# A fused sorted-attention and star-ReLU kernel: second query blocks loaded in f32 on the sync queue, last exps spread before their row sums

## Chip, cores and metric

One core of a Trainium2 chip runs the whole program. The metric is the device time in microseconds of one execution. The kernel before takes 223.7 us (median of three runs, 223.66 to 227.12).

## What is computed

Four batches with eight heads, 768 tokens in eight blocks of 96, head size 64. A small matrix per head (8x8) is normalised five times by exps, rows and columns; it mixes the blocks of keys and values. Each query block attends to its own mixed block. The result goes through a two-layer network with a squared ReLU.

```python
P = sort_net                                   # (4, 8, 8, 8)
for _ in range(5):
    P = exp(P - max(P, -1)); P /= sum(P, -1); P /= sum(P, -2)
k_sorted = einsum('bhij,bhjcd->bhicd', P, k_blocks)      # v the same
attn = softmax(q_block @ k_sorted_block.T / sqrt(64))
x = (attn @ v_sorted_block), heads joined       # 3072 x 512
h = x @ w_in                                   # 512 -> 2048
out = (s * relu(h)**2 + b) @ w_out             # 2048 -> 512
```

Inputs and output are f32. The kernel works in bf16 with f32 sums; the `b` term enters as a bias from the column sums of `w_out`.

## The kernel before

The order on each engine is written by hand: instructions run on an engine in the order in which the code records them, and waits are put in where tiles are shared. A half batch (384 tokens) is one network tile `t`; there are eight.

**The front** (L76 to L263). `sort_net` lies as 32 rows (batch and head) of 64. ACT takes the exps (L213), DVE the sums, reciprocals and products (L218 to L226); between them ACT moves f32 values into place (L183). In the fifth round the last step is the row product (L220); the column division is done later, in `take_p`. PE runs empty products meanwhile (`warm`, L176). `spread_p` (L234) then multiplies the 32 rows with a 0/1 matrix `emat`, so that each of 128 partitions (head, block, half) has its head's matrix: one product per batch, in f32, each two passes. `take_p` (L253) picks the partition's column with a mask, divides it by its sum, and `build_pd` (L275) makes the moving matrix `PD` of the mixing products. The copy `PB` keeps the other batches for later.

**Batch 0** (L550 to L578). `k_piece` (L290) makes 16 of 48 key columns a time: 32 products into a PSUM buffer, and one move to `KS` by ACT ("A") or DVE ("D"). `v_piece`, `q_piece` (transposes of query blocks 0 to 3), scores (`s_piece`), weighted values (`p_piece`) and transposes of x follow. PSUM has three double buffers (tag "a") and two single ones (tag "b"), taken in turn.

**GpSimd** issues nearly all loads, cast from f32 to bf16 on the way: keys, then query blocks 0 to 3 (`load_q(0, range(HB))`, L135), and after the masks are there `load_w` (L141):

```python
nc.gpsimd.tensor_copy(out=ones[:, 0:1], in_=PD[0][:, 0, 0, 0:1])   # holds GpSimd until PD is there
nc.gpsimd.memset(KS[1][:, :, :, C2:GAP], 0.0)
nc.gpsimd.memset(sel, 0.0)
part(0, 0)
nc.gpsimd.tensor_copy(out=ones[:, 0:1], in_=KS[0][:, 0, 0, C2 - 1:C2])  # until the keys are moved
part(0, 1); part(2, 0)
load_q(0, range(HB, NB))       # query blocks 4 to 7, four DMAs
part(2, 1)
```

`part(a, f)` loads rows `a`, `a+1` (of four groups of 128) and column quarter `f` of `w_in`; quarters 2 and 3 and four pieces of `w_out` follow. [...]

**The network** (`ffn1`, L484): for each pair of 128 hidden columns, part 0 and 1 of the four products, then ReLU on ACT (`rt`) and square on DVE (`gt`). `slots` says which other work stands where. In tile 0 (L641) three pairs are begun ahead; `("pre", 1)` and `1` hold `q_blocks` (L327): PE transposes of query blocks 4, 5 and 6, 7, moved by DVE and by ACT. They come ahead of the second half of pair 2, which needs `part(2, 1)`. `sel` and `part` (L584 to L589) are small masks that `sum_w` and `make_bias` use at tile 1.

**The sync engine** issues `sort_net`, four value loads, and from 54 us on transposes and stores.

Of the kernel before, what the change touches and what calls it, by code (L numbers as in the profile page):

```python
# [9 lines left out]
FP = mybir.dt.float32  # L10
BF = mybir.dt.bfloat16
AF = mybir.ActivationFunctionType
ALU = mybir.AluOpType
AX = mybir.AxisListType


def spread(t, dims):

    return bass.AP(tensor=t.tensor, offset=t.offset, ap=[list(t.ap[0])] + dims)
# [3 lines left out]
def kernel(  # L23
# [12 lines left out]
    nc = tc.nc  # L36

    B, H, S, D = q.shape
    NB = sort_net.shape[-1]
    BLK = S // NB  # L40
    BH = B * H
# [4 lines left out]
    HB = NB // 2  # L46
    TG = HB * BLK
    C2 = BLK // 2
# [5 lines left out]
    CK = 16  # L54
# [7 lines left out]
    const = ctx.enter_context(tc.tile_pool(name="const", bufs=1))  # L62
# [5 lines left out]
    rtp = ctx.enter_context(tc.tile_pool(name="rtp", bufs=3))  # L68
    gtp = ctx.enter_context(tc.tile_pool(name="gtp", bufs=2))
    osb = ctx.enter_context(tc.tile_pool(name="osb", bufs=3))  # L70
    psa = ctx.enter_context(tc.tile_pool(name="psa", bufs=3, space=bass.MemoryType.PSUM))
# [6 lines left out]
    sn = sne[:, 0:NB, :]  # L78
# [3 lines left out]
    for c in range(0, C2, CV):  # L82
        nc.sync.dma_start(out=v0f[:, c:c + CV, :].rearrange("p c d -> p (c d)"),
                          in_=raw[2][0][:, c * D:(c + CV) * D])
# [18 lines left out]
    QTOK = {}  # L103

    def load_q(b, ns=range(NB)):

        if b not in QTOK:
            QTOK[b] = rawp.tile([BLK, NB, H, D], BF, tag="rawq", name="qtok")
        qv = q[b].rearrange("h (n t) d -> t n h d", n=NB)
        for n in ns:  # L110
            nc.gpsimd.dma_start(out=QTOK[b][:, n], in_=qv[:, n])  # L111
# [5 lines left out]
    KS = [const.tile([128, NG, 2, GAP], BF, name=f"ks{i}") for i in range(2)]  # L117
# [17 lines left out]
    load_q(0, range(HB))  # L135
    ones = const.tile([128, 32], BF)
    sel = const.tile([128, 128], BF)
    wi = const.tile([128, NHP, d_ff], BF)
    wo = const.tile([128, NF, d_model], BF)

    def load_w():  # L141
        wiv = moe_w_in.rearrange("(a p) f -> p a f", p=128)
        fq = d_ff // 4

        def part(a, f):
            nc.gpsimd.dma_start(out=wi[:, a:a + 2, f * fq:(f + 1) * fq],  # L146
                                in_=wiv[:, a:a + 2, f * fq:(f + 1) * fq])


        nc.gpsimd.tensor_copy(out=ones[:, 0:1], in_=PD[0][:, 0, 0, 0:1])  # L150
        nc.gpsimd.memset(KS[1][:, :, :, C2:GAP], 0.0)
        nc.gpsimd.memset(sel, 0.0)
        part(0, 0)
        nc.gpsimd.tensor_copy(out=ones[:, 0:1], in_=KS[0][:, 0, 0, C2 - 1:C2])
        part(0, 1)
        part(2, 0)
        load_q(0, range(HB, NB))
        part(2, 1)
        for f in (2, 3):
            for a in (0, 2):  # L160
                part(a, f)
        wov = moe_w_out.rearrange("(f p) n -> p f n", p=128)
        for c in range(4):
            fs = slice(c * (NF // 4), (c + 1) * (NF // 4))
            nc.gpsimd.dma_start(out=wo[:, fs, :], in_=wov[:, fs, :])
# [6 lines left out]
    def warm(n, w=512):  # L172
        for _ in range(n):
            if not Z:
                Z.append(psb.tile([128, 512], FP, tag="b", name="z"))
            nc.tensor.matmul(out=Z[0][:, 0:w], lhsT=zeros[:, 0:128], rhs=zeros[:, 0:w],  # L176
                             start=True, stop=True)


    def permute(eng, src, cs=slice(0, C2), ds=slice(0, D)):  # L180
# [25 lines left out]
        for z in range(2)  # L206
# [1 line left out]
    nc.vector.tensor_reduce(out=rstat, in_=sn, axis=AX.X, op=ALU.max)  # L208
    nc.vector.tensor_tensor(out=sn, in0=sn, in1=rstat.broadcast_to([BH, NB, NB]),
                            op=ALU.subtract)  # L210
    warm(108, 142)
    for it in range(5):
        nc.scalar.activation(out=sn, in_=sn, func=AF.Exp)  # L213
        for c in {1: (0,), 2: (1,), 4: (2, 3)}.get(it, ()):
            permute(nc.scalar, v0f, slice(c * CV, (c + 1) * CV))
        if it >= 1:
            idle[it - 1]()
        nc.vector.tensor_reduce(out=rstat, in_=sn, axis=AX.X, op=ALU.add)  # L218
        nc.vector.reciprocal(out=rrec, in_=rstat)
        nc.vector.tensor_tensor(out=sn, in0=sn, in1=rrec.broadcast_to([BH, NB, NB]), op=ALU.mult)  # L220
        if it == 4:
            break
        nc.vector.tensor_reduce(out=rstat, in_=sne.rearrange("p i j -> p j i"),  # L223
                                axis=AX.X, op=ALU.add)
        nc.vector.reciprocal(out=rrec, in_=rstat)
        nc.vector.tensor_tensor(out=sn, in0=sn, in1=spread(rrec, [[0, NB], list(rrec.ap[1])]),  # L226
                                op=ALU.mult)
# [1 line left out]
    PD = {}  # L229
    PT = const.tile([128, B, NB], FP)  # L230
    RC = const.tile([128, B], FP)
    PB = const.tile([128, B - 1, NB, NB], FP)

    def spread_p(b0, n):  # L234

        pe = psa.tile([128, n, NB, NB], FP, tag="a", name="pe")
        for b in range(n):
            nc.tensor.matmul(out=pe[:, b].rearrange("p i j -> p (i j)"), lhsT=emat[:, b0 + b, :],
                             rhs=sn.rearrange("p i j -> p (i j)"), start=True, stop=True)
        return pe  # L240

    def masks_z():
        idz = ident.rearrange("p (z a e j) -> p z a e j", z=2, a=NHP, e=2)
# [9 lines left out]
    def take_p(b0, n, pe, sel):  # L253

        bs = slice(b0, b0 + n)
        tmp = rtp.tile([128, n * NB, NB], FP, tag=f"tmp{n}", name="tmp")
        nc.vector.tensor_tensor(out=tmp, in0=pe.rearrange("p b i j -> p (b i) j"),
                                in1=spread(sel, [[0, n * NB], list(sel.ap[1])]), op=ALU.mult)
        nc.vector.tensor_reduce(out=PT[:, bs].rearrange("p b i -> p (b i)"), in_=tmp, axis=AX.X,
                                op=ALU.add)  # L260
        cs = rtp.tile([128, n], FP, tag=f"cs{n}", name="cs")
        nc.vector.tensor_reduce(out=cs, in_=PT[:, bs], axis=AX.X, op=ALU.add)
        nc.vector.reciprocal(out=RC[:, bs], in_=cs)  # L263
# [26 lines left out]
    def k_piece(b, c0, eng):  # L290
        src, mov, dst = RAW["k", b], PD[b], KS[b % 2]
        ps = psa.tile([128, CK, 2, NG], FP, tag="a", name="tp")
        for c in range(CK):
            for e in range(2):
                nc.tensor.matmul(out=ps[e * 64:(e + 1) * 64, c].rearrange("p z g -> p (z g)"),  # L295
                                 lhsT=src[:, c0 + c, :],
                                 rhs=mov[:, e].rearrange("p z g -> p (z g)"),
                                 start=True, stop=True)
        if b > 1:
            dst = dst.rearrange("p g z c -> p g (z c)")[:, :, 0:BLK].rearrange(  # L300
                "p g (z c) -> p g z c", z=2)
        evac(eng, dst[:, :, :, c0:c0 + CK], ps.rearrange("p c z g -> p g z c"))
# [181 lines left out]
    def ffn1(t, slots, ahead=0):  # L484

        gt = gtp.tile([128, NF, TG], BF, tag="gt", name="gt")
        GT[t] = gt
        xt = XT[t]
        H1 = {}

        def part(i, hpl):
            if i not in H1:
                H1[i] = psa.tile([128, 2, 512], FP, tag="a", name="hps")
            for f in range(2):
                for hp in hpl:
                    fc = (2 * i + f) * 128
                    nc.tensor.matmul(out=H1[i][:, f, 0:TG], lhsT=wi[:, hp, fc:fc + 128],  # L497
                                     rhs=xt[:, :, hp, :],
                                     start=(hp == 0), stop=(hp == NHP - 1))

        for i in range(ahead):
            for p in slots.get(i - ahead, ()):
                p()
            part(i, (0, 1))
        for i in range(NF // 2):
            part(i, (2, 3) if i < ahead else range(NHP))
            for p in slots.get(("pre", i), ()):
                p()
            rt = rtp.tile([128, 2, TG], BF, tag="rt", name="rt")
            h = H1.pop(i)[:, :, 0:TG]  # L510
            nc.scalar.activation(out=rt, in_=h, func=AF.Relu)  # L511
            nc.vector.tensor_tensor(out=gt[:, 2 * i:2 * i + 2, :], in0=rt, in1=rt, op=ALU.mult)  # L512
            for p in slots.get(i, ()):
                p()
# [32 lines left out]
        nc.sync.dma_start(out=out[r0:r0 + 128, ns], in_=ot[:, ns])  # L547


    take_p(0, 1, spread_p(0, 1), jsel)  # L550
    build_pd(0)
    pe = spread_p(1, B - 1)
    nc.vector.tensor_copy(out=PB, in_=pe)
    warm(3)
    k_piece(0, 0, "A")
    k_piece(0, CK, "D")
    k_piece(0, 2 * CK, "A")
    load_w()
    v_piece(0, 0, "A")
    q_piece(0, 0, "D")  # L560
# [23 lines left out]
    part = const.tile([128, 2], FP)  # L584
    nc.gpsimd.memset(part, -1.0)
    for r in range(0, 128, 32):
        nc.gpsimd.memset(sel[r:r + 3], 1.0)
        nc.gpsimd.memset(part[r:r + 1, 0:1], 0.0)
        nc.gpsimd.memset(part[r:r + 2, 1:2], 0.0)  # L589
    nc.gpsimd.memset(VO, 1.0)  # L590
# [44 lines left out]
    def TP(b, h, i, eng): return lambda: t_piece(b, h, i, eng)  # L635
    def TD(b, h): return lambda: t_dma(b, h)
    def PDB(b): return lambda: build_pd(b)
    def QB(b, n0, eng): return lambda: q_blocks(b, n0, eng)


    ffn1(0, {-1: [TP(0, 0, 2, "AD")], ("pre", 1): [QB(0, HB, "D")], 1: [QB(0, HB + 2, "A")],  # L641
             2: [SB(0, 1, 0)], 3: [SB(0, 1, 1), P(0, 1, 0)], 4: [SB(0, 1, 2), P(0, 1, 1)],
             5: [SB(0, 1, 3), P(0, 1, 2)], 6: [TP(0, 1, 0, "D"), P(0, 1, 3)]}, ahead=3)
    ffn1(1, {-2: [TP(0, 1, 2, "D")], 1: [masks_z, lambda: take_p(1, B - 1, PB, jselz), PDB(1)], 4: [PDB(2), sum_w],
# [20 lines left out]
    for b in range(B):  # L665
        n = b + 1
# [55 lines left out]
```

## Time and profile before

| | us |
|---|---|
| median of three runs | 223.7 |
| the profiled execution, its own time | 224.31 |
| its span, first to last instruction | 222.5 |
| PE busy | 214.8 (97%) |
| DVE / ACT / GpSimd busy | 116.6 / 100.8 / 55.2 |
| first key product on PE | 12.79 |
| transposes of query blocks 4 to 7 on PE | 26.67 to 27.5 |
| second half of pair 2, tile 0 | 28.44 |
| last `wo` piece seen landed | 43.7 |

The span is that of one profiled execution; the rest of its own time lies before the first and after the last instruction that the profile shows. PE is busy nearly all the time at its full granted clock, so the share alone says only that little is left; where PE waits is read from the timeline. The GpSimd queue's loads and their times, from issue until the landing is seen:

| load | issued | landed after |
|---|---|---|
| `part(0, 0)` | 14.04 | 4.0 |
| `part(0, 1)` | 16.15 | 5.9 |
| query blocks 4 to 7 | 17.55 to 20.6 | 6.0 to 6.5 |
| `part(2, 1)` | 20.62 | 7.8 |
| pieces of `wo` | 25.0 to 29.4 | 11.1 to 15.0 |

The column "DMA" of a queue's share is the sum of the times of its packets over 16 engines; packets overlap, so it can exceed 100%.

### The profile page before, as it was taken

The page shows a single profiled execution, that of the slowest core. Times are in us where ns is not written, and L with a number is a line of the kernel's source. Part 1 is how long each engine was busy: PE and PEld are TensorE (multiplying, and loading weights), DVE is VectorE, ACT ScalarE, POOL GpSimd, SP SyncE. Part 2 cuts the span into 40 slices and gives each one's busy share as a digit, 9 for nine tenths or more (in the row PEclk, how much of TensorE's full clock was granted, in tenths as well). Part 3 has the DMA queues.
Part 4 walks back from the last instruction along what each step waited for, and adds up shares of the span by engine and source line. Part 5 has one row for each costly group of instructions (what it writes and reads, how often), then busy time and mean ns, then how long its engine had stood idle before and what let it go on. Part 6 is the DMA issues. An engine that isn't in the chain of part 4 may idle for free.

```text
span 222.5 us, 5383 instructions
## 1 busy us (share of the span) xinstructions
PE 214.8 (97%) x2307; PEld 127.1 (57%) x2307; DVE 116.6 (52%) x237; ACT 100.8 (45%) x132; POOL 55.2 (25%) x99
## 2 busy tenths in 40 slices
PE   7898889999999999999999999999999999999993
PEld 8886556655555545655555545665455566654453
DVE  6857547599938556443426746444244734442122
ACT  4688476565442326663354136664325055650000
POOL 8349787359030009100040019000000000000000
PEclk9999999999999999999999999999999999999999
DMA  5999999999979769999669869969423240001212
GB/s 178 258 95 131 163 203 207 219 193 132 177 137 219 147 165 122 156 112 211 160 134 202 209 155 141 151 133 207 114 78 72 102 111 4 0 0 47 94 50 94
DMA packets 66744, 30.51 MB, mean 137 GB/s; under 512 B 57440, under 2 KB 61920, under 8 KB 66528
## 3 DMA queue, kind: packets, MB, share of 16 engines
q0 software_dynamic: 30832, 12.85, 47.3%
q1 hardware_dynamic: 35888, 17.31, 34.4%
q8 instruction: 18, 0.29, 0.5%
q14 instruction: 6, 0.05, 0.1%
HBM read 29.63 MB, written 8.65 MB: 172 GB/s over the span
## 4 chain that ended last, share of the span: by engine, by line
PE 86%; DMA 4%; DVE 4%; POOL 2%; ACT 2%; issue 1%; POOLq 0%
PE ops L522 36%; PE hps L497 36%; DMA wi<-in_moe_w_in_dram 3%; PE pv L441 3%; PE tp L295 2%; PE sc L406 2%; PE ops L536 2%; POOL qtok L111 1%; PE tv L379 1%; ACT ks L284 1%; DMA sne<-in_sort_net_dram 1%; POOL wi L146 1%; PE vob L360 1%; ACT sne L213 1%; DVE rstat L223 1%
## 5 line engine op out<-in xcount | busy, mean ns | idle before, releaser
L497 PE MATMUL hps<-xt,wi 128*128 128x384 bf16 x512 | 86.4, 326 | 1.3 <-DMA wi<-in_moe_w_in_dram 0.9
L522 PE MATMUL ops<-wo,gt 128*128 128x512 bf16 x368 | 84.9, 379 | 0.0
L511 ACT ACTIVATE rt<-hps 128x768 bf16<-128x768 f32 x64 | 51.6, 811 | 52.9 <-PE hps L497 52.0
L497 PEld LDWEIGHTS <-wi 128*128 128x128 bf16 x512 | 48.9, 98 | 35.4 <-issue 2.5
L512 DVE TENSOR_TENSOR gt<-rt 128x768 bf16<-128x768 bf16 x64 | 38.4, 602 | 44.0 <-ACT rt L511 41.9
L522 PEld LDWEIGHTS <-gt 128*128 128x128 bf16 x368 | 34.0, 98 | 37.6
L544 DVE SCALAR_TENSOR_TENSOR ot<-ops,s_bc,bias 128x512 f32<-128x512 f32 (+2 forms) x26 | 18.4, 706 | 33.5 <-PE ops L522 31.5
L411 ACT ACTIVATE at<-sc 96x768 bf16<-96x768 f32 (+1 forms) x28 | 21.2, 806 | 28.4 <-PE sc L406 28.4
L111 POOL DMA_DIRECT2D qtok<-in_q_dram x32 | 24.8, 786 | 7.5 <-DMA wo<-in_moe_w_out_dram 3.7
L449 DVE TENSOR_TENSOR x<-pv,rec 96x512 bf16<-96x512 f32 x32 | 22.0, 687 | 1.1
L441 PEld LDWEIGHTS <-at 112*128 112x128 bf16 (+3 forms) x256 | 10.9, 101 | 4.3 <-ACT vs L284 0.9
L441 PE MATMUL pv<-vs,at 112*128 112x66 bf16 (+3 forms) x256 | 11.7, 195 | 0.8 <-DVE vs L286 0.8
L176 PE MATMUL z<-zeros 128*128 128x142 bf16 (+1 forms) x114 | 11.0, 268 | 1.2 <-DVE zeros L115 1.2
L448 DVE RECIPROCAL rec<-pv 96x8 f32<-96x8 f32 x32 | 6.3, 198 | 11.2 <-PE pv L441 11.2
L284 ACT CAST ks<-tp 128x1024 bf16<-128x1024 f32 x8 | 8.1, 1012 | 7.4 <-PE tp L295 7.4
L176 PEld LDWEIGHTS <-zeros 128*128 128x128 bf16 x114 | 9.5, 116 | 1.4 <-DVE zeros L114 1.0
L661 POOL COPY gate<-gt 128x1 bf16<-128x1 bf16 x2 | 0.4, 191 | 36.8 <-DVE gt L512 36.8
L406 PEld LDWEIGHTS <-ks 64*128 64x128 bf16 x224 | 5.2, 94 | 5.1 <-issue 2.1
L286 DVE CAST ks<-tp 128x1024 bf16<-128x1024 f32 x4 | 4.9, 1222 | 5.7 <-PE tp L295 5.7
L406 PE MATMUL sc<-qt,ks 64*128 64x96 bf16 x224 | 7.5, 204 | 0.2 <-DVE x L449 0.2
L295 PEld LDWEIGHTS <-rawk 128*64 128x64 bf16 x384 | 6.4, 113 | 1.7 <-issue 1.3
L295 PE MATMUL tp<-pd,rawk 128*64 128x64 bf16 x384 | 6.8, 196 | 0.0
(105 smaller groups left out, 117.9 us busy)
## 6 DMA issues: line engine op xcount, KB each, us to landing
out_dram<-ot SPq DMA_DIRECT2D x23, 256.0 KB, 2.1
qtok<-in_q_dram POOLq DMA_DIRECT2D x32, 96.0 KB, 7.2
rawk<-in_k_dram POOLq DMA_DIRECT2D x6, 384.0 KB, 10.3
rawv<-in_v_dram POOLq DMA_DIRECT2D x6, 384.0 KB, 6.6
dv<-VO SPq DMA_DIRECT2D x12, 192.0 KB, 6.4
vs<-dv SPq DMA_DIRECT2D x2, 1152.0 KB, 7.2
wi<-in_moe_w_in_dram POOLq DMA_DIRECT2D x8, 256.0 KB, 8.1
wo<-in_moe_w_out_dram POOLq DMA_DIRECT2D x4, 512.0 KB, 13.8
```

Of the source, the lines that this page charges most:

```text
L111: nc.gpsimd.dma_start(out=QTOK[b][:, n], in_=qv[:, n])
L176: nc.tensor.matmul(out=Z[0][:, 0:w], lhsT=zeros[:, 0:128], rhs=zeros[:, 0:w], start=True, stop=True)
L295: nc.tensor.matmul(out=ps[e * 64:(e + 1) * 64, c].rearrange("p z g -> p (z g)"), lhsT=src[:, c0 + c, :], rhs=mov[:, e].rearrange("p z g -> ...
L406: nc.tensor.matmul(out=sc[:, e, n * BLK:(n + 1) * BLK], lhsT=KS[b % 2][pr, g0 + n].rearrange("p z c -> p (z c)"), rhs=QT[b][pr, half * HB ...
L411: nc.scalar.activation(out=at, in_=sc[0:rows(b), :, 0:TG], func=AF.Exp, scale=scale)
L441: nc.tensor.matmul(out=pv[0:m, e, n * VW:(n + 1) * VW], lhsT=atf[:, c0:c0 + m], rhs=VS[b > 1][:, e * NG + g0 + n, 0:VW], start=True, stop= ...
L449: nc.vector.tensor_tensor(out=x[:, :, hp * 128:(hp + 1) * 128].rearrange("p n (e d) -> p e n d", e=2), in0=pvv[:, :, :, 0:D], in1=rec.unsq ...
L497: nc.tensor.matmul(out=H1[i][:, f, 0:TG], lhsT=wi[:, hp, fc:fc + 128], rhs=xt[:, :, hp, :], start=(hp == 0), stop=(hp == NHP - 1))
L511: nc.scalar.activation(out=rt, in_=h, func=AF.Relu)
L512: nc.vector.tensor_tensor(out=gt[:, 2 * i:2 * i + 2, :], in0=rt, in1=rt, op=ALU.mult)
L522: nc.tensor.matmul(out=ops, lhsT=gt[:, f, m * 128:(m + 1) * 128], rhs=wo[:, f, :], start=(f == 0), stop=(f == NF - 1))
L544: nc.vector.scalar_tensor_tensor(out=ot[:, ns], in0=ops, scalar=s_bc, in1=BIAS[0][:, ns], op0=ALU.mult, op1=ALU.add)
```

## The change

Four things are changed together.

1. In the fifth round the row product is dropped. The exps themselves are spread as soon as ACT has made them, for all batches; the reciprocals of the row sums are spread by further products (`spread_r`) into a ninth row of the same PSUM buffers, and `take_p` multiplies by them. `PB` keeps nine rows. Four fewer empty products run before.
2. Query blocks 4 to 7 are loaded in f32, by four DMAs on the sync engine's queue, into a new tile `q0f`. A GpSimd memset of a part of `q0f`, after `part(0, 1)`, is what these DMAs wait for. Two DVE casts write the bf16 tile; they stand in slot -1 of tile 0, after the transposes of x.
3. GpSimd no longer waits for the moved keys between `part(0, 0)` and `part(0, 1)`; the four row memsets of `sel` move ahead of `part(0, 0)`.
4. The first three key moves go to DVE, ACT, DVE, where they went to ACT, DVE, ACT.

```diff
+    q0f = const.tile([BLK, HB, H, D], FP)
...
         nc.gpsimd.memset(sel, 0.0)
+        for r in range(0, 128, 32):
+            nc.gpsimd.memset(sel[r:r + 3], 1.0)
         part(0, 0)
-        nc.gpsimd.tensor_copy(out=ones[:, 0:1], in_=KS[0][:, 0, 0, C2 - 1:C2])
         part(0, 1)
+        nc.gpsimd.memset(q0f[:, :, 0, 0:1], 0.0)
+        qv = q[0].rearrange("h (n t) d -> t n h d", n=NB)
+        for n in range(HB):
+            nc.sync.dma_start(out=q0f[:, n], in_=qv[:, HB + n])
         part(2, 0)
-        load_q(0, range(HB, NB))
         part(2, 1)
...
-    warm(108, 142)
+    warm(104, 142)
...
-        nc.vector.tensor_tensor(out=sn, in0=sn, in1=rrec.broadcast_to([BH, NB, NB]), op=ALU.mult)
         if it == 4:
             break
+        nc.vector.tensor_tensor(out=sn, in0=sn, in1=rrec.broadcast_to([BH, NB, NB]), op=ALU.mult)
...
+    def spread_r(b0, n, pe):
+        for b in range(n):
+            nc.tensor.matmul(out=pe[:, b, NB], lhsT=emat[:, b0 + b, :], rhs=rrec,
+                             start=True, stop=True)
...
-        nc.vector.tensor_reduce(out=PT[:, bs].rearrange("p b i -> p (b i)"), in_=tmp, axis=AX.X,
-                                op=ALU.add)
+        pt = rtp.tile([128, n, NB], FP, tag=f"pt{n}", name="pt")
+        nc.vector.tensor_reduce(out=pt, in_=tmp, axis=AX.X, op=ALU.add)
+        nc.vector.tensor_tensor(out=PT[:, bs], in0=pt, in1=pe[:, :, NB], op=ALU.mult)
...
-    take_p(0, 1, spread_p(0, 1), jsel)
+    pe0 = spread_p(0, 1)
+    pe = spread_p(1, B - 1)
+    spread_r(0, 1, pe0)
+    spread_r(1, B - 1, pe)
+    take_p(0, 1, pe0, jsel)
     build_pd(0)
-    pe = spread_p(1, B - 1)
     nc.vector.tensor_copy(out=PB, in_=pe)
     warm(3)
-    k_piece(0, 0, "A")
-    k_piece(0, CK, "D")
-    k_piece(0, 2 * CK, "A")
+    k_piece(0, 0, "D")
+    k_piece(0, CK, "A")
+    k_piece(0, 2 * CK, "D")
...
-        nc.gpsimd.memset(sel[r:r + 3], 1.0)
...
+    def cast_q(n):
+        nc.vector.tensor_copy(out=QTOK[0][:, HB + n:HB + n + 2], in_=q0f[:, n:n + 2])
...
-    ffn1(0, {-1: [TP(0, 0, 2, "AD")], ("pre", 1): [QB(0, HB, "D")], 1: [QB(0, HB + 2, "A")],
+    ffn1(0, {-1: [TP(0, 0, 2, "AD"), lambda: cast_q(0), lambda: cast_q(2)], ("pre", 1): [QB(0, HB, "D")], 1: [QB(0, HB + 2, "A")],
```

More of the change, by code (lines that the diff above doesn't have):

```diff
@@ L231 @@
     RC = const.tile([128, B], FP)
-    PB = const.tile([128, B - 1, NB, NB], FP)
+    PB = const.tile([128, B - 1, NB + 1, NB], FP)
     def spread_p(b0, n):
-        pe = psa.tile([128, n, NB, NB], FP, tag="a", name="pe")
+        pe = psa.tile([128, n, NB + 1, NB], FP, tag="a", name="pe")
         for b in range(n):
-            nc.tensor.matmul(out=pe[:, b].rearrange("p i j -> p (i j)"), lhsT=emat[:, b0 + b, :],
+            nc.tensor.matmul(out=pe[:, b, 0:NB].rearrange("p i j -> p (i j)"), lhsT=emat[:, b0 + b, :],
                              rhs=sn.rearrange("p i j -> p (i j)"), start=True, stop=True)
         return pe
+    def spread_r(b0, n, pe):
+        for b in range(n):
+            nc.tensor.matmul(out=pe[:, b, NB], lhsT=emat[:, b0 + b, :], rhs=rrec,
+                             start=True, stop=True)
     def masks_z():
@@ L255, in take_p @@
         bs = slice(b0, b0 + n)
-        tmp = rtp.tile([128, n * NB, NB], FP, tag=f"tmp{n}", name="tmp")
-        nc.vector.tensor_tensor(out=tmp, in0=pe.rearrange("p b i j -> p (b i) j"),
-                                in1=spread(sel, [[0, n * NB], list(sel.ap[1])]), op=ALU.mult)
-        nc.vector.tensor_reduce(out=PT[:, bs].rearrange("p b i -> p (b i)"), in_=tmp, axis=AX.X,
-                                op=ALU.add)
+        tmp = rtp.tile([128, n, NB, NB], FP, tag=f"tmp{n}", name="tmp")
+        nc.vector.tensor_tensor(out=tmp, in0=pe[:, :, 0:NB],
+                                in1=spread(sel, [[0, n], [0, NB], list(sel.ap[1])]), op=ALU.mult)
+        pt = rtp.tile([128, n, NB], FP, tag=f"pt{n}", name="pt")
+        nc.vector.tensor_reduce(out=pt, in_=tmp, axis=AX.X, op=ALU.add)
+        nc.vector.tensor_tensor(out=PT[:, bs], in0=pt, in1=pe[:, :, NB], op=ALU.mult)
         cs = rtp.tile([128, n], FP, tag=f"cs{n}", name="cs")
```

## The prediction

> **What bounds the kernel now.** I read first the engine table and the slices (PE busy 97%, granted clock full everywhere), then the chain of waits, then the timeline around each place where PE stands, then the DMA queues in one-microsecond windows. The chain, in order of time, passes here (start us, length us, what):
>
> ```profile
> 11.04 1.07 PE pe L238 x8
> ...
> 15.69 0.19 POOL ones L154
> ...
> 16.15 1.42 POOL wi L146 x2
> 17.57 3.06 POOL qtok L111 x4
> 20.62 7.77 DMA wi<-in_moe_w_in_dram
> ```
>
> From 28.4 us to the end it is almost only PE. So there are two places to gain: the front up to the first key products, and the 0.93 us in which PE waits for the weight quarter `part(2, 1)` that GpSimd issues behind four query loads. Anything that makes PE wait after that is paid in full. The timeline shows what stands there (start, length, engine, line, operation; in brackets idle time and its releaser):
>
> ```profile
> 24.87 0.36 DVE L286 COPY xt<-tr 128x384 bf16<-128x384 bf16 x1 [0.52 <-PE tr L469]
> 26.67 0.85 PE L333 MATMUL tqb<-ident,qtok 96*128 96x96 bf16 x16
> 27.06 0.56 DVE L512 TENSOR_TENSOR gt<-rt 128x768 bf16<-128x768 bf16 x1 [1.84 <-ACT rt L511]
> 28.44 0.82 PE L497 MATMUL hps<-xt,wi 128*128 128x384 bf16 x4 [0.93 <-DMA wi<-in_moe_w_in_dram]
> ```
>
> PE transposes the second query blocks at 26.67. In the changed kernel that transpose stands behind two DVE casts, and they behind four loads on the sync queue. So the question is when those loads land. It is answered by how the two queues share the 16 DMA engines. These are the queue lines of four windows of 1 us, from 6, 29, 85 and 88 us (packets, MB, share of 16 engines; q0 is GpSimd's queue, q1 the sync engine's):
>
> ```profile
> q0 software_dynamic: 57, 0.12, 61.3%
> q1 hardware_dynamic: 57, 0.18, 47.7%
> ...
> q0 software_dynamic: 192, 0.18, 115.8%
> ...
> q1 hardware_dynamic: 886, 0.17, 89.6%
> ...
> q0 software_dynamic: 445, 0.06, 84.3%
> q1 hardware_dynamic: 452, 0.09, 77.1%
> ```
>
> At 6 us (key pieces against the f32 value load) and at 88 us (query rows against the rows stored for v) both queues are busy, and each gets the same number of packets although their sizes differ. The windows at 121 and 122 us, with 6 KB packets on q0 and 2 KB on q1, show 37 against 31 and 28 against 30. So they take turns packet by packet, and a queue with small packets gets few bytes beside one with large packets.
>
> [...] at 88 us a q1 packet takes 77.1% x 16 us / 452 = 27 ns, against 89.6% x 16 / 886 = 16 ns alone at 85 us, so nearly every single packet meets one of the other queue. [...] The nearest row here, the cast of 128x512 f32 at 48.77 us, took 0.43[...].
>
> **Queries on the sync queue (decides).** Removed from GpSimd: four issues, 3.06 us, ahead of `part(2, 1)`. Added on the sync engine: four issues, about 0.43 us each (the f32 value loads), behind a small GpSimd memset, and on DVE two casts. Nothing waits on the sync queue behind them until the key and query transposes at 53.9 us.
>
> When do they start? GpSimd's first weight issue was at 14.04; four small memsets of `sel` come ahead of it (0.20 each as a row at 29.50, partly overlapped: 0.6 to 0.8), the front moves it by -0.2 to 0 (below): 14.6. Two issues of 0.71 follow back to back, since the `KS` gate is gone, then the memset: 16.2. Sync issues at 16.3; its first packets come 0.6 us (the v rows, issued 82.87, running at 83.5) to 1.8 us after (the value load, issued 1.2, at full rate from 3.0). I take 17.5.
>
> How long? Before, the same query rows were 768 packets a load (24,576 of q0's 30,832 packets are 32 such loads). In f32 they are still runs of 64 elements, so four loads are 3,072 packets, 192 on each engine. GpSimd's queue meanwhile holds eight weight parts of 256 packets and four of `wo` with 512: 256 on each engine, so it does not run dry. One turn is a weight packet and a query packet. A weight packet alone costs 16 us / 192 = 83 ns, a small sync packet alone 16 us / 886 = 18 ns: 101 ns. From above, their durations beside each other: 115.8% x 16 / 192 = 97 and 27, 124 ns. At 6 us the turn of 16 / 57 = 281 ns lay between these two ways of counting (172 + 134 = 306). I take 105 ns. 192 turns are 20.2 us (19.4 to 23.8). The last load ends at 37.7, and is seen about 0.8 us later (value loads: last packets near 9.5 us, landing at 10.3): **38.5 us**. The first two are seen near 28.4.
>
> What waits? Both casts stand on DVE ahead of the first `gt` product (27.06), of the evacuation of the transposed queries (27.54) and of the second `gt`. Had the data been there by 25.2, they would lie in DVE's 1.84 us of idle time and cost nothing[...]. As it is, the second ends at 39.2. PE, in order, stands at the second `tqb` of eight transposes (0.42 us), and behind it part 2 of ffn1, which began at 28.44 and now begins at 39.7: **+11.2 us**, with the old 0.93 us wait swallowed. ACT and DVE are free to catch up in PE's stall, the rest behind it is PE's own chain, so nothing is given back. GpSimd's next loads keep their place: the same DMA engines have carried the same read bytes by then, and the batch-1 queries, issued from 41.77 before, also wait for `tqb` at 39.7.
>
> Bounds: if one engine's gaps let query packets through (q0 moved only 117 to 148 packets per us at 16 to 27 us, against 192 to 214 later), up to 9 us are saved; at 124 ns a turn, 3.6 us are added.
>
> **Front.** The row product (0.21 us) and its wait leave the path: PE waits for the exps, which end at 10.19, not for 10.90, so the first `pe` comes at about 10.34 instead of 11.04 (`warm` at 104 ends at 9.9). But `spread_r` stands behind all eight passes of `spread_p` (1.0 us), so the reciprocals arrive near 11.65, and one more product of 128x8 (about 0.16, the reduction of that size) follows: masks some 0.2 us earlier. Against it PE runs eight more passes (0.12 each, 1.0 us if the weight loads set the pace) and then `warm(3)`, 0.8 us: the key products start near 13.05 instead of 12.79. The swap gives the first key move to DVE (1.23 us against 1.01), which frees the buffer that the first v products wait for later: +0.2. Sum +0.3 to +0.5, bounded by -0.4 (if the passes overlap) and +0.7. All of it lies in the shadow of the query wait and costs nothing; without that wait it counts. `PB` has 24 columns more and the later `take_p` one op more (0.18 us on DVE at 45 us), beside PE work: nothing, at worst 0.2.
>
> **Sum.** Profiled span 222.5 + 11.2 = 233.7; its own time 224.31 + 11.2 = 235.5. That run lies 0.6 us above the median of 223.7, from which 234.9 follows: I say **235**.
>
> **Rivals.** *Hidden*: the queues share by bytes or time, or sync packets go in bunches. Four loads of 0.8 MB against an equal share of weights end 5 us after the start, by 24 us; the casts fit in the idle time, `part(2, 1)` lands 3 to 4 us earlier and PE's 0.93 us wait goes, the front gives back 0.3 to 0.5: 223.2 (222.5 to 224), not slower. [...] against it: the equal counts. It decides if the loads land before about 26 us. *Gaps*: the slow rate at 16 to 27 us means that engines wait for descriptors, and the other queue fills in; landing at 28 to 33, +1 to +6: 225 to 230. For it: the rates above; against: the slowest of 16 engines ends a load, and one without gaps is enough. *Front only*: the early spread does nothing because PE is in order; with hidden queries 223.7 + 0.4 - 0.9, within the first rival's range.
>
> **Chances.** One for one 0.80 (own range 230 to 239), gaps 0.07, hidden 0.13. The range 227 to 239 holds the first but for its ends and half of the second: about 0.8. Two per cent, 4.5 us, is what a measurement of this kernel can tell from no change (its three runs span 1.5%). Slower by over 2% is one-for-one and a little of gaps: 0.81. Within 2%: 0.18. Faster would need 219.2, below what PE's own work leaves (214.8 busy in 222.5 and 0.93 to win): 0.01.
>
> **What would show it.** A DVE wait of more than 10 us ahead of the casts, released by the q0f loads; PE idle until near 39 us; equal packet counts of both queues from 18 to 38 us, with q1 near 150 packets per us; q0f landing 10 to 20 us after issue. It is wrong if q1 shows several times q0's count in that stretch, or if the first relu products keep their time at 27 us. The front is right if the first key product starts at 12.6 to 13.1.

## The result, and the profile after

The changed kernel takes **243.35 us** (median of six runs, 240.6 to 246.86), the kernel before 224.62 beside it (223.48 to 227.12). The runs of the changed kernel lie near 241 or near 246, and every ratio here compares the shorter runs of both kernels: 1.072, interval 1.064 to 1.081. That is some 16 us more; forecast were 11 us more, 235, and a range up to 239. The direction was right, the size was 5 us too small by this ratio.

The profiled execution's own time is 245.52, its span 243.7; against it the forecast was 10 us too small. Of its profile these are the span, the engines' busy time, the PE slices with the granted clock, and the two DMA queues:

```profile
span 243.7 us, 5396 instructions
...
PE 219.3 (90%) x2311; PEld 128.8 (53%) x2311; DVE 120.0 (49%) x241; ACT 100.0 (41%) x131; POOL 51.8 (21%) x95
...
PE   8797411994999999999999999999999999999994
...
PEclk9999955598999999999999999999999999999999
...
q0 software_dynamic: 27696, 12.46, 40.5%
q1 hardware_dynamic: 39024, 18.10, 34.1%
```

The same two rows of the kernel before:

```profile
PE   7898889999999999999999999999999999999993
...
PEclk9999999999999999999999999999999999999999
```

PE does 4.5 us more of busy time and still falls from 97% to 90%. A slice is 6.1 us. Slices 5 to 7 of the PE row (4, 1, 1) are one hole from about 27 to 42 us, and the clock row reads 5 in slices 6 to 8: half speed, where the kernel before has 9, full speed, throughout. Slice 10 has a second, smaller dip in both rows. The chain of waits shows what the hole is (start us, length us, what; the SPq rows are the sync engine's issues):

```profile
16.88 0.11 POOL q0f L158
...
17.01 0.34 SPq L161
...
17.40 0.54 SPq L161
...
17.98 2.67 SPq L161
...
20.69 20.47 DMA q0f<-in_q_dram
...
41.19 0.70 DVE qtok L656
...
41.93 0.82 PE tqb L345 x8
```

Before, the chain passed here through GpSimd's issues and a weight quarter, and came out at 28.4. Now it is the last of the four query loads, one transfer of 20.5 us. The sync engine took 2.67 us for the third issue and 5.02 for the fourth, where 0.43 was expected. The timeline shows both casts, and a second place where PE stands:

```profile
31.25 1.76 DVE L656 CAST qtok<-q0f 96x1024 bf16<-96x1024 f32 x1 [5.51 <-DMA q0f<-in_q_dram]
41.19 0.69 DVE L656 CAST qtok<-q0f 96x1024 bf16<-96x1024 f32 x1 [8.18 <-DMA q0f<-in_q_dram]
...
33.07 0.82 PE L345 MATMUL tqb<-ident,qtok 96*128 96x96 bf16 x8 [5.72 <-DVE qtok L656]
41.93 0.82 PE L345 MATMUL tqb<-ident,qtok 96*128 96x96 bf16 x8 [8.05 <-DVE qtok L656]
42.55 1.48 PE L509 MATMUL hps<-xt,wi 128*128 128x384 bf16 x4
...
54.35 3.77 DVE L524 TENSOR_TENSOR gt<-rt 128x768 bf16<-128x768 bf16 x1 [0.56 <-ACT rt L523]
54.58 3.11 POOL L190 COPY VP<-rawv 128x384 bf16<-128x384 bf16 x4
...
58.64 1.46 PE L509 MATMUL hps<-xt,wi 128*128 128x384 bf16 x4 [3.26 <-DVE xt L298]
```

The brackets carry the reading: DVE waits 5.5 and 8.2 us for the loads, PE 5.7 and 8.05 us for the casts, and the second half of pair 2 starts at 42.55 where it started at 28.44. It stands behind the transposes in the code and waits there although what it reads was there long before: the last `xt` piece was copied by 25.74, and all quarters of `wi` had landed by 33.4 (last issue 20.4, longest landing 13.0). The last three lines are a loss that the prediction did not have: a `gt` product that takes about 0.56 us elsewhere takes 3.77, lies beside GpSimd's moves of `VP`, and holds up the DVE copy `xt` behind it, for which PE waits 3.26.

The account of the added span, by stage. Beside it stands the profile of **e2**, which has the query part of the change alone; that execution took 240.99:

| us | changed kernel | e2 |
|---|---|---|
| second half of pair 2 starts later | 14.1 (42.55 - 28.44) | 14.2 (42.62 - 28.44) |
| the next two pairs at half clock (3.02 before) | 2.4 (5.41) | 1.1 (4.13) |
| PE waits behind a `gt` held up by GpSimd | 3.3 | 1.5 |
| half clock once more behind that wait (7.02 before) | 1.6 (8.59) | none |
| sum | 21.4 | 16.8 |
| span less 222.5 | 21.2 | 16.7 |

The second row compares 42.55 to 47.96 (e2: 42.62 to 46.75) with 28.44 to 31.46 before, the fourth 58.64 to 67.23 with 38.80 to 45.82 before. The first row is the same in both columns. The next three are 7.3 us in one profile and 2.6 in the other; what sets the two executions apart is not shown.

### The profile page after: what moved, and what is told of

The parts are those of the page before. It is cut to its first block, busy times and chain, and to the rows that moved or that the text cites. A ratio compares the mean times of both kernels' runs of the same rounds, so it can differ in the third digit from the quotient of the medians.

```text
span 243.7 us, 5396 instructions
## 1 busy us (share of the span) xinstructions
PE 219.3 (90%) x2311; PEld 128.8 (53%) x2311; DVE 120.0 (49%) x241; ACT 100.0 (41%) x131; POOL 51.8 (21%) x95
## 3 DMA queue, kind: packets, MB, share of 16 engines
q0 software_dynamic: 27696, 12.46, 40.5%
q1 hardware_dynamic: 39024, 18.10, 34.1%
## 4 chain that ended last, share of the span: by engine, by line
PE 80%; DMA 9%; DVE 5%; ACT 1%; SPq 1%; POOL 1%; issue 1%; POOLq 0%
PE hps L509 34%; PE ops L534 33%; DMA q0f<-in_q_dram 8%; PE pv L453 3%; PE sc L418 2%; PE tp L307 2%; DVE gt L524 2%; SPq L161 1%; PE ops L548 1%; PE tv L391 1%; DMA sne<-in_sort_net_dram 1%; ACT VP L188 1%; PE scb L433 1%; POOL wi L147 1%; PE vob L372 1%
## 5 line engine op out<-in xcount | busy, mean ns | idle before, releaser
L509 PE MATMUL hps<-xt,wi 128*128 128x384 bf16 x512 | 89.8, 334 | 3.5 <-DVE xt L298 3.3
L509 PEld LDWEIGHTS <-wi 128*128 128x128 bf16 x512 | 50.0, 100 | 39.1 <-issue 5.0
L556 DVE SCALAR_TENSOR_TENSOR ot<-ops,s_bc,bias 128x512 f32<-128x512 f32 (+2 forms) x26 | 18.4, 706 | 33.8 <-PE ops L534 31.5
L423 ACT ACTIVATE at<-sc 96x768 bf16<-96x768 f32 (+1 forms) x28 | 21.2, 805 | 28.4 <-PE sc L418 28.4
L111 POOL DMA_DIRECT2D qtok<-in_q_dram x28 | 21.6, 783 | 8.7 <-DVE gt L524 2.5
L345 PE MATMUL tqb<-ident,qtok 96*128 96x96 bf16 x16 | 1.6, 278 | 13.8 <-DVE qtok L656 13.8
L460 DVE RECIPROCAL rec<-pv 96x8 f32<-96x8 f32 x32 | 6.3, 196 | 11.2 <-PE pv L453 11.2
L181 PE MATMUL z<-zeros 128*128 128x142 bf16 (+1 forms) x110 | 9.8, 254 | 1.2 <-DVE zeros L115 1.2
L296 ACT CAST ks<-tp 128x1024 bf16<-128x1024 f32 x7 | 7.1, 1012 | 8.2 <-PE tp L307 8.2
L298 DVE CAST ks<-tp 128x1024 bf16<-128x1024 f32 x5 | 6.0, 1223 | 6.6 <-PE tp L307 6.6
L656 DVE CAST qtok<-q0f 96x1024 bf16<-96x1024 f32 x2 | 2.4, 1224 | 13.7 <-DMA q0f<-in_q_dram 13.7
L181 PEld LDWEIGHTS <-zeros 128*128 128x128 bf16 x110 | 8.3, 109 | 1.4 <-DVE zeros L114 1.0
L345 PEld LDWEIGHTS <-qtok 96*128 96x128 bf16 x16 | 1.2, 135 | 14.4 <-DVE qtok L656 14.4
```

The costliest lines, as they stand in the source:

```text
L296: nc.scalar.copy(out=out, in_=in_)
L423: nc.scalar.activation(out=at, in_=sc[0:rows(b), :, 0:TG], func=AF.Exp, scale=scale)
L556: nc.vector.scalar_tensor_tensor(out=ot[:, ns], in0=ops, scalar=s_bc, in1=BIAS[0][:, ns], op0=ALU.mult, op1=ALU.add)
```

## The experiments

### Which part: e1 without the sync loads, e2 with them alone

e1 is the changed kernel with the second queries back on GpSimd:

```diff
-        nc.gpsimd.memset(q0f[:, :, 0, 0:1], 0.0)
-        qv = q[0].rearrange("h (n t) d -> t n h d", n=NB)
-        for n in range(HB):
-            nc.sync.dma_start(out=q0f[:, n], in_=qv[:, HB + n])
         part(2, 0)
+        load_q(0, range(HB, NB))
...
-    {-1: [TP(0, 0, 2, "AD"), lambda: cast_q(0), lambda: cast_q(2)], ...
+    {-1: [TP(0, 0, 2, "AD")], ...
```

> The changed kernel with query blocks 4 to 7 back on GpSimd's queue ahead of part(2, 1), and no casts; spread, swap, sel and the dropped key gate stay. Theory (the sync queue's query loads are the whole loss): 223.5 to 224.5 us, first key product near 13.2, part 2 of ffn1 held by the weight load as before. Rival (the new front carries part of the loss): over 226.

Measured: 224.97 against 224.66, ratio 1.0024 [0.9995, 1.0052]. The front, the swap and the removed gate together cost 0.5 us, with an interval from -0.1 to 1.2.

e2 is the kernel before with the same loads and casts added that e1 takes away.

> The kernel before with only the queries moved to the sync queue and cast on DVE; front, key gate and swap as before. Theory: 239 to 243 us like the changed kernel, last q0f load seen at 40 to 42 us, casts behind it. Rival (the loss needs the new front or the dropped key gate): under 230.

Measured: 243.29 (240.99 to 246.27), ratio 1.0727 [1.0641, 1.0813], the changed kernel's own ratio. Its timeline:

```profile
42.00 0.82 PE L337 MATMUL tqb<-ident,qtok 96*128 96x96 bf16 x8 [7.98 <-DVE qtok L647]
...
54.91 2.62 DVE L516 TENSOR_TENSOR gt<-rt 128x768 bf16<-128x768 bf16 x1
...
58.05 4.71 PE L501 MATMUL hps<-xt,wi 128*128 128x384 bf16 x28 [1.49 <-DVE xt L290]
```

The same stall, and the second wait again, but shorter. The queries on the sync queue make the whole loss; the rest of the change is worth nothing that these runs can tell from zero.

### Turns of the queues: e4, e7

Both queues in two windows of 1 us of the changed kernel, from 24 and 30 us (packets, MB, share of 16 engines):

```profile
q0 software_dynamic: 155, 0.15, 89.0%
q1 hardware_dynamic: 155, 0.04, 30.9%
...
q0 software_dynamic: 160, 0.15, 90.6%
q1 hardware_dynamic: 159, 0.04, 29.8%
```

Equal counts: 16 us / 155 = 103 ns for a turn of one weight packet and one query packet. What the profile counts as a packet is here about one row: with the four loads of 768 rows, 3,136 packets went from q0 (30,832 to 27,696) to q1 (35,888 to 39,024). Equal counts over 1 us would also come from long turns of equal length, but in the ten windows of 0.1 us from 24 to 25 us each queue has 14 to 18 packets every time, about one for each of the 16 engines, and with long turns sixteen engines would hardly stay so even. This speaks for one to one.

The counts were not equal from the start:

```profile
q0 software_dynamic: 121, 0.12, 72.0%
q1 hardware_dynamic: 381, 0.10, 49.7%
```

That is the window from 22 us; the one before it has 94 and 243. After 38 us q1 fades to 96, 46 and 18 per us, and the last load is seen landed at 41.16. The likely reading, which no view by engine shows, is that some engines were done with their small packets earlier than others, and that the load waited for the last one.

If turns and not bytes are the cost, fewer packets for the same bytes must take the loss away. e4 reads 2 KB runs, 384 packets in place of 3,072; the blocks 4 to 7 then hold other rows of `q`:

```diff
-        qv = q[0].rearrange("h (n t) d -> t n h d", n=NB)
+        qv = q[0].rearrange("h (n t) d -> (h n t d)", n=NB).rearrange("(n p w) -> p n w", n=2 * HB, w=H * D)
         for n in range(HB):
-            nc.sync.dma_start(out=q0f[:, n], in_=qv[:, HB + n])
+            nc.sync.dma_start(out=q0f[:, n].rearrange("p h d -> p (h d)"), in_=qv[:, HB + n])
```

> The changed kernel with the four sync loads taking the same number of bytes into the same tile, at the same place, but from contiguous runs of 2 KB instead of 256 B: 384 packets or fewer instead of 3,072. It reads other rows of q, so query blocks 4 to 7 hold other values. Theory (turns are by packet, not by bytes): last load seen 5 to 8 us after the first issue at 17, by 25; no PE wait, 222.7 to 224.5 us. Rival (shared by bytes, or sync loads held back altogether behind GpSimd's): last load still near 40, 238 to 243 us.

Measured: 224.83 in the median of twenty, ratio 1.0002 [0.9977, 1.0027]. The window from 24 us, and the timeline:

```profile
q0 software_dynamic: 102, 0.09, 55.8%
q1 hardware_dynamic: 99, 0.18, 52.6%
```

```profile
27.54 0.69 DVE L656 CAST qtok<-q0f 96x1024 bf16<-96x1024 f32 x1 [0.35 <-DMA q0f<-in_q_dram]
...
28.72 0.82 PE L509 MATMUL hps<-xt,wi 128*128 128x384 bf16 x4
```

Counts are nearly equal again, with over four times the bytes per us on q1. The last load is seen at 27.5 instead of 41.2, and PE waits for nothing at 28.72. The mechanism is shown: the number of packets against a queue that never runs dry. The time is 0.3 us above the expectation. In the profile the first network product stood at 24.19 instead of 23.34: the granted clock was half from 12.2 to 15.6 us, and the first key products took 2.50 instead of 1.71.

e7 does it for the first two loads only; blocks 4 and 5 hold other rows:

```diff
+        ql = q[0].rearrange("h s d -> (h s d)").rearrange("(n p w) -> p n w", n=2 * HB, w=H * D)
         for n in range(HB):
-            nc.sync.dma_start(out=q0f[:, n], in_=qv[:, HB + n])
+            if n < 2:
+                nc.sync.dma_start(out=q0f[:, n].rearrange("p h d -> p (h d)"), in_=ql[:, HB + n])
+            else:
+                nc.sync.dma_start(out=q0f[:, n], in_=qv[:, HB + n])
```

> The changed kernel with the first two sync loads from contiguous runs of 2 KB, the other two in rows of 256 B: 12 + 96 packets on each engine instead of 192 (or 24). Query blocks 4 and 5 hold other values. Theory (each packet costs one turn of about 107 ns): last load seen at 20.9 + 108 x 0.107 + 0.7, about 33, between 25.4 and 41; part 2 at 34.3 to 35, 5.5 to 6.5 us behind the run with long rows, with what the clock adds 229.5 to 232 us. Rival (a threshold, not a count): near 224.7 or near 240.

Measured: 237.38 (237.03 to 238.57), ratio 1.0577 [1.0508, 1.0645]: between e4 and the changed kernel, but 5 us above what was expected. Windows from 22 and 28 us:

```profile
q0 software_dynamic: 103, 0.10, 61.5%
q1 hardware_dynamic: 97, 0.17, 48.8%
...
q0 software_dynamic: 159, 0.16, 92.1%
q1 hardware_dynamic: 161, 0.04, 30.1%
```

Turns with 2 KB packets take 16 / 97 = 165 ns in the first window, those with 256 bytes 100 ns in the second, and the first packet came near 21.3. The last landing was seen at 35.5, part 2 began at 37.09. From there the two later losses came on top, as in the changed kernel: the next two pairs in 5.3 instead of 3.0 us, and a wait of 2.44 for DVE, which two `gt` products beside GpSimd's moves had put behind (4.18 us for both). The expectation had 107 ns for every turn, and nothing for that wait.

### The second loss: e5

GpSimd's four value moves (L190) are left out; part of batch 1's value tile keeps old contents.

```diff
     load_q(1)
-    for i in (0, 1, 2, 4):
-        permute(nc.gpsimd, RAW["v", 1], ds=slice(i * 8, (i + 1) * 8))
```

> The changed kernel without GpSimd's four value moves for batch 1 (L190): half of that batch's value tile keeps old contents. Theory (the gt product of 3.8 us at 54 us is held by GpSimd's copies, which before fell beside other DVE work): that product takes 0.56, PE's wait behind it (3.3 us in the profile shown, 1.5 in the queries-only run) goes, 1 to 3.5 us less than the changed kernel, so 237.5 to 240 us in runs like its 240.5 to 241. Rival (held by GpSimd's query loads or by the DMA traffic): the product stays above 2 us and the time as it was.

Measured: 240.1 (238.94 to 240.55), ratio 1.068 [1.061, 1.075]. The `gt` of the same place:

```profile
55.88 0.56 DVE L524 TENSOR_TENSOR gt<-rt 128x768 bf16<-128x768 bf16 x1
```

0.56 instead of 3.77, and PE has no wait after 42.28. That the moves held the product is shown. The gain in time is small: 0.8 us below 240.9, the middle of the changed kernel's runs near 241, with intervals that overlap, and just above the expected 237.5 to 240. In the profile part 2 begins at 42.90 and the next two pairs take 4.8 us, so 14.5 us of stall and 1.8 of slow products make up its 16.1 us over the kernel before: what the product gave back, the start and the clock took in part.

By what means a copy holds the product is not shown. What the traces show is 3.77 and 2.62 us beside copies and 0.56 beside the memset of `VO`, and that an earlier start did not help: the product starts first (54.35 against 54.58) and ends at 58.12, after all four copies (57.69). A `gt` was slow beside the copies before, too (3.41); these are two lines of the kernel before, the first beside the memset, the second beside the copies:

```profile
31.83 0.56 DVE L512 TENSOR_TENSOR gt<-rt 128x768 bf16<-128x768 bf16 x1 [1.12 <-ACT rt L511]
...
51.69 3.41 DVE L512 TENSOR_TENSOR gt<-rt 128x768 bf16<-128x768 bf16 x1 [0.24 <-ACT rt L511]
```

PE then had other work ahead of it, 2.75 us of `ops` from 50.86 and 1.71 us of `tp` behind it, and did not wait. GpSimd's moves came 2.4 us later than before (54.58 for 52.15) and the network 14, so they met another place of it.

### The half clock: e6

Empty products of 512 columns (24 and 36) are put ahead of the two groups of query transposes, so that PE is not idle (`WARM` calls `warm` with a buffer of its own):

```diff
...
-    ("pre", 1): [QB(0, HB, "D")], 1: [QB(0, HB + 2, "A")],
+    ("pre", 1): [WARM(24), QB(0, HB, "D")], 1: [WARM(36), QB(0, HB + 2, "A")],
```

> The changed kernel with 24 empty products of 128x512 on PE ahead of the transposes of query blocks 4, 5 and 36 ahead of those of 6, 7, about 5.1 and 7.7 us, which fit into the stall. Theory (standing still for 14 us costs PE its clock, and it restarts at half for 2 to 6 us): granted clock stays full from 28 to 50 us, two pairs of hidden columns after the stall take 3.0 us as before instead of 4.1 to 5.4, runs near 239 us, and fewer near 246. Rival (the slow products come from something else, such as the weights): no change.

Measured: 242.27 (240.41 to 246.26), ratio 1.0757 [1.0665, 1.085]: no gain in time that can be told, and not the expected 239. Engine tables from 42 to 46 and 46 to 50 us (stretch, length, busy time and count of PE, weight loads, DVE, ACT, GpSimd, then the clock, DMA share, GB/s), first of the changed kernel, then of e6:

```profile
42.00:46.00 4.00, 4.00 (x26) 2.05 (x27) 1.83 (x4) 2.37 (x4) 0.81 (x1) 0.50 1.23 218
46.00:50.00 4.00, 4.00 (x43) 2.17 (x42) 1.36 (x3) 1.96 (x4) 2.98 (x4) 0.72 1.02 209
```

```profile
42.00:46.00 4.00, 2.97 (x30) 1.71 (x30) 1.91 (x4) 2.27 (x4) 0.81 (x1) 1.00 1.20 218
46.00:50.00 4.00, 4.00 (x55) 2.43 (x56) 2.43 (x6) 3.15 (x6) 3.56 (x5) 1.00 1.05 216
```

The clock stays at 1.00 and the two pairs take 3.3 us again: that PE's standing cost the clock is shown. But the empty products take one of two PSUM buffers, so the second transposes wait until the first ones have been moved out and began 1.0 us later (42.94), and the wait behind the held `gt` was 2.18. So the gain was given back, and the runs cannot price the clock alone.

The clock records have half speed for 17.1 us from 31.2 in the changed kernel, 3.8 us after PE had stopped at 27.35, and for 13.7 us from 31.5 in e2, 4.6 us after PE had stopped at 26.94. Full speed came back 6.3 us after the restart near 42 in the one and 3.2 in the other; what sets these delays is not shown. So the same stall cost 2.4 us in one profile and 1.1 in the other.

### Loads earlier: e3, e8, e9

e3 is the changed kernel with the memset of `q0f` and the sync loads moved ahead of the memset of `KS[1]`, so ahead of all weights.

> The changed kernel with the same four sync loads let go earlier, ahead of the memset of KS[1] instead of after part(0, 1), so that they fall into the stretch from 14 to 17 us where the DMA engines carry almost nothing. Theory (turns with weight packets make them late): last load seen by 17 to 23 us, casts in DVE's idle time near 26, PE's wait gone, 222.7 to 224.5 us. Rival (the sync queue's loads of 64-element rows, or the casts, are slow in themselves): over 230.

Measured: 224.68, 227.21, 231.74 and 235.16; these four runs do not settle the time. What the profile, of the run of 224.68, shows is clear. The window from 15 us:

```profile
q1 hardware_dynamic: 1001, 0.25, 111.9%
```

With nothing on q0, the small packets go at 1,001 per us instead of 155, so they are not slow in themselves. The loads, issued from 13.5 to 15.6, landed after 3.1 to 6.2 us, as expected; the casts followed at 26.5 without a wait.

e8 puts the same early loads into the kernel before:

> The kernel before with the queries on the sync queue, let go as soon as the masks are there, and cast on DVE; front, swap and key gate as before. Theory: loads land by 20, casts in DVE's idle time, part(2, 1) earlier by the four query issues, PE's wait of 0.9 us gone, and none of the new front's 0.3 to 0.5: 222.7 to 223.7 us against 223.5 to 224.6 of the kernel before. Rival (the weights start late behind the queries and give the gain back): 224 or more.

Measured: 230.31 in the median of 21 (223.57 to 235.5), ratio 0.9984 [0.9937, 1.0031]: no gain, and 13 of the 21 runs took 228 us or more. The expected 222.7 to 223.7 was missed. The profile, of a run of 229.59, again has DVE held by GpSimd:

```profile
50.12 3.45 DVE L623 CAST cbits<-cfull 128x512 bf16<-128x512 f32 x1
50.13 3.15 POOL L189 COPY VP<-rawv 128x384 bf16<-128x384 bf16 x4
...
54.48 0.38 PE L630 MATMUL bps<-cbits,sel 128*128 128x512 bf16 x1 [2.33 <-DVE cbits L624]
```

e9 is e8 with these moves held until the last `gt` of tile 1 is there:

```diff
     load_q(1)
-    for i in (0, 1, 2, 4):
-        permute(nc.gpsimd, RAW["v", 1], ds=slice(i * 8, (i + 1) * 8))
...
+    def pool_moves():
+        nc.gpsimd.tensor_copy(out=gate[:, 0:1], in_=GT[1][:, NF - 1, 0:1])
+        for i in (0, 1, 2, 4):
+            permute(nc.gpsimd, RAW["v", 1], ds=slice(i * 8, (i + 1) * 8))
...
-             7: [make_bias, lambda: permute(nc.vector, RAW["v", 1], ds=slice(40, D))]}, ahead=3)
+             7: [make_bias, lambda: permute(nc.vector, RAW["v", 1], ds=slice(40, D)), pool_moves]}, ahead=3)
```

> The kernel before with the queries on the sync queue right behind the masks (as in e8), and GpSimd's four value moves held until the last gt product of tile 1 is written. Theory (early loads let GpSimd's moves start at 50 us instead of 52, onto DVE's cast at 50.1, which then took 3.45 us and held PE for 2.3): no DVE instruction over 1.5 us between 45 and 56 us, no PE wait there, 222.7 to 223.7 us where the kernel before has 223.5 to 224.6. Rival (the long runs of e8, 228 to 235 us, come from the start of the program, not from these moves): the spread of its runs stays, median over 226.

Measured: 225.4 in the median of 24 (223.59 to 231.66), ratio 1.003 [1.0001, 1.0058]: neither the theory's 222.7 to 223.7 nor the rival's 226. The moves now stand at 60.85, and DVE is not held there; but in the profile, of the run of 231.66, it is held elsewhere:

```profile
28.69 5.12 DVE L645 CAST qtok<-q0f 96x1024 bf16<-96x1024 f32 x2
...
28.71 3.94 POOL L594 MEMSET VO<- 128x4608 bf16 x1
```

The casts, 0.69 each when free, run into the memset of `VO` (the first takes 4.5), and PE waits 2.84 us for them. No version is shown to beat the kernel before.

### The front: e10

In e1 the first mask product waits until batch 0's part of `spread_r` has run, because the reciprocals lie in the same PSUM tile as the exps. e10 is e1 with batch 0's reciprocals in a tile of their own:

```diff
-        nc.vector.tensor_tensor(out=PT[:, bs], in0=pt, in1=pe[:, :, NB], op=ALU.mult)
+        nc.vector.tensor_tensor(out=PT[:, bs], in0=pt, in1=pe[:, :, NB] if r is None else r, op=ALU.mult)
...
-    spread_r(0, 1, pe0)
+    r0 = psb.tile([128, 1, NB], FP, tag="b", name="r0")
+    nc.tensor.matmul(out=r0[:, 0], lhsT=emat[:, 0, :], rhs=rrec, start=True, stop=True)
     spread_r(1, B - 1, pe)
-    take_p(0, 1, pe0, jsel)
+    take_p(0, 1, pe0, jsel, r0)
```

> The run with the queries back on GpSimd (e1), with batch 0's spread reciprocals in a PSUM buffer of their own instead of a ninth row of the one that holds the spread exps. Theory (the mask product, which needs only the exps, waited for the reciprocals because both lie in one tile): that product starts near 10.8 instead of 11.7, the mixing matrix is done 0.2 to 0.3 us earlier, near 12.5; key products stay near 13.1, since PE's spread of reciprocals and three empty products stand ahead of them; time within 0.2 us of e1. Rival (it waits for PE's speed): product still at 11.7.

Measured: 224.74, ratio 1.0019 [0.9996, 1.0042]. The same product in the timeline of e1, then of e10, with PE's lines behind it:

```profile
11.68 0.23 DVE L265 TENSOR_TENSOR tmp<-pe,jsel 128x64 f32<-128x64 f32 x1 [0.96 <-PE pe L247]
```

```profile
10.78 0.23 DVE L265 TENSOR_TENSOR tmp<-pe,jsel 128x64 f32<-128x64 f32 x1
...
12.19 1.19 PE L178 MATMUL z<-zeros 128*128 128x512 bf16 x3
13.31 0.90 PE L304 MATMUL tp<-pd,rawk 128*64 128x64 bf16 x26
```

The mask chain gains 0.9 us at its first product, so the shared tile was the cause, and 0.57 at `pd` (12.22 for 12.79). The key products stay at 13.3: PE is busy with the spreading and `warm(3)` until then. In this profile the granted clock is half from 12.5 to 15.9 us, and the three empty products take 1.19 us instead of the 0.82 of the changed kernel; at full clock PE would be free some 0.4 us earlier, an estimate from these two numbers. So the front has two arms of nearly equal length, and how much the shortened one would give is open; in the time it gives nothing that can be told.

## Why the prediction held where it held, and failed where it failed

**Direction and mechanism: right, and shown.** e2 has the whole loss, e4 takes it away with the same bytes in an eighth of the packets, e7 lies between. The turn was put at 105 ns: the windows have 103 and 100. Most of the named signs came. DVE's wait is split into 5.5 and 8.2 us, neither over 10. The 0.7 us for a cast between 38.5 and 39.2 was the author's estimate, which no trace of the kernel before showed; undelayed casts took 0.68 and 0.69 (e4). The last load landed 20.5 us after its issue, a little beyond the 20 named. And in two windows, from 21 and 22 us, q1 did show some three times q0's count, which was named as a sign of being wrong; the counts were equal from 23 us on, and the last load landed later than forecast all the same.

**The step that failed: the sum ended at the stall, which it also put too short.** "ACT and DVE are free to catch up in PE's stall, the rest behind it is PE's own chain, so nothing is given back." Nothing was given back, but more was lost. 11.2 us were added to the span of 222.5; e2 has 16.7 and the changed kernel's profile 21.2, so 5.5 and 10.0 more:

- *Start of the loads.* 17.5 was taken, from delays of 0.6 to 1.8 us behind the issue. The issue at 17.0 was later than 16.3, one packet came near 20.5, and the stream began at 21.1. The landing was seen at 41.16 for 38.5; with the transposes behind it part 2 began at 42.55 for 39.7: 2.9 us, and 3.0 in e2, where packets came from 19.5 on and the loads landed no earlier. Early loads with GpSimd's queue still nearly empty (e3) had packets 1.0 us after the first issue. What holds them longer behind a filled one was not tried.
- *PE's clock.* No term stood for it. 1.1 us in e2, 4.0 in the changed kernel's profile (2.4 and 1.6). e6 shows the cause of the first part in the trace, not its price in time.
- *The held `gt`.* No term: 1.5 us in e2, 3.3 in the changed kernel's profile. The sentence that GpSimd's "next loads keep their place" was nearly right, and that was the trouble: its moves kept their place too (54.58 for 52.15 before), while the network moved 14 us and they met another place of it. e5 shows that they hold the product. The first cast, beside the memset of `VO`, took 1.76 us instead of 0.70, inside the stall, where it cost nothing.

These are 5.6 for 5.5 in e2, and 10.2 for 10.0 in the changed kernel's profile.

**Two readings were off, without harm.** q0 did not move 117 to 148 packets per us throughout the stretch from 16 to 27 us: it moved 108 from 17 us, and 531 to 1,152 from 21 to 25, while query rows ran. And the stream of the v rows issued at 82.87 begins at 83.7 and is not there at 83.5, so the shorter of the two delays was 0.8 and not 0.6.

**Front: right in sign and size, with one wrong step.** First key product 13.18 against 13.05 forecast (just above the 13.1 of the named sign), first network product 0.5 later (23.34 for 22.83). The masks were to come 0.2 earlier and `pd` came 0.4 later (12.78 for 12.38), for the reason that e10 shows; there it stands at 12.22. By e1 the front, the swap and the gate are worth 0.5 us, with zero inside the interval. The forecast had no clock term here either: of the eight profiles with the new front, six have a stretch of half clock that begins between 11.5 and 13 us, and of the four with the old front none has. Why is not shown.

**The rivals.** "Hidden" is what e4 becomes when the number of packets falls, at 224.83, with 224.66 for the kernel before beside it, for the 222.5 to 224 given against 223.7. "Gaps" fell: landing near 41, not 28 to 33, though small packets went through faster early (381 per us from 22 us, 155 from 24); the counts that fade after 38 us fit the objection that the prediction made itself, that the slowest of 16 engines ends a load. The 0.93 us that PE waited for `part(2, 1)` is gone in e4's profile, but the network began 1.4 us later there than before (24.19 for 22.83), and nothing is left of it in the time.

**Open.** Runs of e3, e8 and e9 reach 231 to 235, two runs each of e4 and e10 and one of the kernel before 230 to 233. The profiles of e8 and e9 have a PE pause of 1.2 us that ends at 19.2 to 19.3 us with no releaser, and stretches of half clock; no run tells their cause.

## What to carry to other kernels

Count packets, not bytes, before a load is moved to another queue beside a full one: here each of 192 small packets on an engine paid for a large one, 103 ns for the two. Add to a stall of PE what follows it: the clock that it costs (1.1 us in e2's profile, 4.0 in the changed kernel's), and engines that kept going and now meet other work (1.5 and 3.3). An early load beside a quiet queue was quick here (3.1 to 6.2 us to landing in e3), but the old place had hidden the load already, and no gain was seen.

## What was not expected of the hardware

- Two queues shared the engines with equal counts of packets, as far as these windows show one to one: 155 to 155 with 1 KB against 256 bytes, 102 to 99 with 2 KB.
- The DVE cast from f32 to bf16 was slow beside a GpSimd memset (0.69 becomes 1.76, and 5.12 for two in e9), while the `gt` product took 0.56 beside the same memset.
- Sync loads issued from 17.0 us on, with GpSimd's queue filled, showed one packet some 3.5 us later and a stream from 4.1 us on (2.4 in e2); the third and fourth issue took 2.67 and 5.02 us. With that queue nearly empty (e3) the first packets came after 1.0 us.
